# The first batch's attention as float32 matmuls on 64 x 64 quarters of the array, two heads at once

## The chip, the cores and the metric

The program runs on one NeuronCore of a Trainium2 chip. The metric is the device time of one execution in microseconds, median of several runs; lower is better. In the text PE is TensorE, PEld its weight loads, ACT is ScalarE, DVE is VectorE, POOL is GpSimd, and SP is the engine that issues nearly all DMAs of this kernel.

## What is computed

Three stages follow one another: a sigmoid attention, a gated feed-forward block behind an RMS norm, and a top-1 mixture of eight experts. The change touches the first stage alone, and of that the first of four batches.

```python
# q, k, v: (4 batches, 12 heads, 448 tokens, 64), float32
def _attn_ref(q, k, v):
    scores = np.matmul(q, k.transpose(0, 1, 3, 2)) / np.sqrt(64) - np.log(448)
    return np.matmul(1.0 / (1.0 + np.exp(-scores)), v)

def _moe_ref(x, w_gate, w_val, w_out, rms_g):     # x: (1792, 768), d_ff 1536
    xn = x / np.sqrt(np.mean(x * x, axis=-1, keepdims=True) + 1e-06) * rms_g
    g = xn @ w_gate
    return (g / (1.0 + np.exp(-g)) * (xn @ w_val)) @ w_out
# then _moe2_ref: logits = x @ w_gate; the best expert's relu(x @ w1) @ w2, times its probability
```

## The kernel before

One program in an order written out by hand issues everything; every engine works through its own queue in that order. The four batches pass through two stages that overlap. `attention(b)` is a generator whose steps are one chunk of keys of one head (12 heads, NC = 4 chunks of 128 keys, the last one of 64). `moe1(b)` is the feed-forward block of a batch in steps of nine matmuls, and between its steps it calls steps of the next batch's attention. The first batch's attention has nothing to run beside, so it stands alone at the start of the program, and beside it run the conversions of the first twelve chunks of the feed-forward weights (HELD = 12).

**Queries and keys.** `load_qk` fetches a head's 128 x 960 tile `rqk` (480 KB): the 64 dimensions of its queries and keys, twice over, one copy under the other. `prep` makes three things of it: an ACT cast of the whole tile to the matmul type float32r (`qkh`, L528), a DVE subtraction that puts the queries' rest into the lower 64 partitions (L530), and a DVE subtraction for the keys' rest (`kl`, L532). `scores` then runs two float32r matmuls for a chunk, L556 and L557, over all 128 rows.

**Values.** In the first batch `whole` is true for all six pairs of heads: the weights `a` and the raw values `rv` (352 KB for a pair, padded with zeros so that two heads share one 128-column result) go into plain float32 matmuls, L602 for a full chunk and L604 for the two short chunks of a pair at once. `combine_pair` copies the result to `xt` by ACT (L636), and `squares` adds its squares to `ss` (ACT L630, DVE L631).

**Weights.** `load_64` fetches one of the 36 chunks of 768 KB as 64-bit words into one of three buffers, `narrow` makes float32 of it in three DVE operations (L227, L231, L235). The load for the third chunk after it is queued on SP some ticks behind the last of the three. `split_w` makes of two converted chunks the operands `wh` and `wl` of the first feed-forward step (ACT L258, DVE L261).

**The end of the first attention.** When `ss` is complete, four small matmuls `pm` (L700) sum it over partitions, DVE takes the inverse root (L705 to L728), matmuls `prs` (L732) spread it over partitions, and six rounds of DVE and ACT work make the operands `xh` and `xl` of `moe1(0)`. Meanwhile the first steps of batch 1's attention are taken, one for each of these steps.

SP issues DMAs in the order of the program, and each of them waits for its buffer: a waiting DMA holds all that stand behind it.

Of the kernel before, what the change touches and what calls it, by code (L numbers as in the profile page):

```python
# [19 lines left out]
B, H, S, D = 4, 12, 448, 64  # L20
# [20 lines left out]
SP = mybir.EngineType.SP  # L41

HELD = 12
HELD_AT = (1, 1, 1, 0)

RAW = 3

# [6 lines left out]

def whole(b, p):

    return b == 0 or b == 1 and p in (0, 2, 4)


def attention_due(b, n):  # L60
# [44 lines left out]
def f32(ap):  # L105
    return ap.bitcast(F32)


@with_exitstack
def block_kernel(ctx, tc, qk, v, vw, wg, wv, wo, g, gate, w1, w2, consts, out):  # L110
    nc = tc.nc
    ctx.enter_context(tc.manual_schedule())

# [59 lines left out]
    def later(ticks, f, *a):  # L173

        due.setdefault(clock[0] + ticks, []).append((f, a))
# [42 lines left out]
    def narrow(c):  # L218

        r = w64.pop(c)  # L220
        lo, hi = r[:, :, 0], r[:, :, 1]
        if place[c] is not None:
            w = wp.tile([128, DM], F32, tag=f"h{place[c]}", name="w32h")
        else:
            w = wp.tile([128, DM], F32, tag="w32", name="w32", bufs=4)
        u = w.bitcast(I32)
        nc.vector.tensor_scalar(  # L227
            out=u, in0=hi, scalar1=3, scalar2=0x3FFFFFF8, op0=ALU.logical_shift_left, op1=ALU.bitwise_and
        )
        yield  # L230
        nc.vector.scalar_tensor_tensor(  # L231
            out=u, in0=lo, scalar=29, in1=u, op0=ALU.logical_shift_right, op1=ALU.bitwise_or
        )
        yield
        nc.vector.scalar_tensor_tensor(  # L235
            out=u, in0=hi, scalar=-0x40000000, in1=u, op0=ALU.bitwise_and, op1=ALU.bitwise_or
        )
        w32[c] = w
        if c < HELD:
            to_store.append((c, w))  # L240
        else:
# [264 lines left out]

    def load_qk(b, h):
        r = aq.tile([128, S + KW], F32, tag="rqk", name="rqk", bufs=RQK)
        nc.sync.dma_start(out=r, in_=qk[b, h])
        raw_a[b, h] = r  # L510

    raw_v = {}
# [1 line left out]
    def load_v(b, p):  # L514
        rv = aq.tile([128, VW], F32, tag="rv", name="rv", bufs=2)
        if whole(b, p):
            nc.sync.dma_start(out=rv, in_=vw[b, p])
        else:
            nc.sync.dma_start(out=rv[:, : 4 * 128], in_=v[b, p])
        raw_v[b, p] = rv  # L520
# [24 lines left out]
    def attention(b):  # L545
# [5 lines left out]
        def scores(t):  # L551
            h, c = divmod(t, NC)
            q2, kh, kl, _ = prep_a[b, h]
            psc = (mm_bank if b == 0 and t % 5 in (1, 3, 4) else sc_bank)([128, S], "psc")
# [107 lines left out]
            for f, a in steps_due.pop(now[0], []):  # L662
                f(*a)

        for t in range(n_steps + 4):
# [24 lines left out]
            next(coming, None)  # L690
            yield
# [403 lines left out]
        yield  # L1095


    load_qk(0, 0)
    load_v(0, 0)
    for h in range(1, RQK):  # L1100
        load_qk(0, h)
    for _ in prep(0, 0):
        pass
    att = {b: attention(b) for b in range(B)}
    for n in range(H * NC + 5):
        next(att[0])
        if n in (2, 4, 6):
            load_64(n // 2 - 1)
        if n == 20:
# [3 lines left out]
        if n == 30:  # L1113
# [7 lines left out]
        if n in (40, 44):  # L1121
            split_w(0, n // 4 - 10)
    ahead_of = 0
    for _ in att[0]:
        tick()
# [155 lines left out]
def _layout(q, k, v, moe_w_gate, moe_w_val, moe_w_out, moe_rms_g, moe2_w_gate, moe2_w1, moe2_w2):  # L1281
    c = np.ascontiguousarray

    words = lambda w: c(w).view(np.int64)
    cols = lambda w: words(w.reshape(KD, 128, KF, 128).transpose(2, 1, 0, 3))


    vp = v.reshape(B, H // 2, 2, S, D)
    parts = np.concatenate([vp, vp[:, :, :, 384:]], axis=3).reshape(B, H // 2, 2, 4, 128, D).transpose(0, 1, 4, 3, 2, 5)
    padded = np.zeros((B, H // 2, 128, VW // D, D), v.dtype)  # L1290
    for c3 in range(3):
        padded[:, :, :, 3 * c3 : 3 * c3 + 3 : 2] = parts[:, :, :, c3]
    padded[:, :, :64, 9] = parts[:, :, :64, 3, 0]
    padded[:, :, 64:, 10] = parts[:, :, 64:, 3, 1]

    once = np.concatenate([q, k, k[:, :, 384:]], axis=2).transpose(0, 1, 3, 2)
    return {
        "qk": c(np.concatenate([once, once], axis=2)),
        "v": c(parts).reshape(B, H // 2, 128, 4 * 128),
        "vw": padded.reshape(B, H // 2, 128, VW),  # L1300
        "wg": cols(moe_w_gate),
        "wv": cols(moe_w_val),
        "wo": words(moe_w_out.reshape(KF, 128, KD, 128).transpose(2, 1, 0, 3)),
        "g": c(moe_rms_g.reshape(KD, 128).T),
        "gate": c(moe2_w_gate.reshape(KD, 128, E).transpose(1, 0, 2)),
        "w1": c(moe2_w1),
        "w2": c(moe2_w2),
        "consts": CONSTS,
    }
# [17 lines left out]
```

## Time and profile before

| | us |
|---|---|
| three runs | 1013.36, 1014.91, 1015.14; median 1014.91 |
| the profiled execution | 1011.73 |
| its span, first to last instruction | 1009.9 |
| first score matmul of batch 0 | 6.17 |
| last value matmul of batch 0 issued | 60.4 |
| `pm` of batch 0 | 65.07 |
| `moe1(0)` in dense work from | 72.8 |

The profile has a busy time for each engine, a chain of work followed back from the last instruction, groups of equal instructions with their mean time, and a timeline. A matmul's record is longer than the time that it keeps the array, since consecutive ones overlap; how long it keeps the array is the distance from one start to the next. A plain float32 matmul leaves two records, a float32r matmul one. PE is in work all through: what can be won is what shortens the stretch before 72.8 us, or makes PE's work less.

### The profile page before, as it was taken

How to read it: one execution, taken by the hardware profiler on the slowest of the kernel's cores; microseconds unless marked ns; L12 is line 12 of the kernel's file. 1: busy time of each engine (PE TensorE's matmuls, PEld its weight loads, DVE VectorE, ACT ScalarE, POOL GpSimd, SP SyncE). 2: the span in 40 equal slices, each digit the busy share in tenths (PEclk: the TensorE clock that was granted, in tenths of full speed). 3: DMA queues.
4: the chain of work that ended last, by engine and by line, in shares of the span. 5: the costliest groups of instructions: out<-in, count | busy, mean ns of one | idle time of the engine just before them, and what ended most of it. 6: DMA issues, size and time to landing. Idle time of an engine off the chain costs nothing.

```text
span 1009.9 us, 13971 instructions
## 1 busy us (share of the span) xinstructions
PE 980.6 (97%) x4998; PEld 868.8 (86%) x4998; DVE 676.1 (67%) x1172; ACT 511.1 (51%) x845; POOL 14.9 (1%) x43
## 2 busy tenths in 40 slices
PE   7989999998999999999999999999999999999995
PEld 5658988897899999989999999999898878889994
DVE  5889987897789785678878465654445834434453
ACT  6865766643788883478888333333322132232230
POOL 0000000010000000000000100000000000000000
PEclk9999999999999999999999999999999999999998
DMA  8987863686735345564432469433576649839542
GB/s 312 348 291 283 322 209 111 221 251 201 229 97 179 112 130 147 168 193 125 151 128 79 142 196 341 126 98 125 152 220 236 183 138 363 296 104 304 156 73 40
DMA packets 123120, 191.48 MB, mean 190 GB/s; under 512 B 62665, under 2 KB 79817, under 8 KB 123040
## 3 DMA queue, kind: packets, MB, share of 16 engines
q1 hardware_dynamic: 122896, 189.95, 58.0%
q8 instruction: 41, 0.67, 0.3%
q0 software_dynamic: 144, 0.53, 0.2%
q14 instruction: 39, 0.32, 0.1%
HBM read 152.44 MB, written 37.88 MB: 188 GB/s over the span
## 4 chain that ended last, share of the span: by engine, by line
PE 89%; DVE 6%; DMA 2%; issue 1%; ACT 1%; SPq 0%; DVEq 0%; ACTq 0%
PE mm L305 20%; PE mm L307 20%; PE mm L306 19%; PE sc L305 4%; PE sc L306 4%; PE sc L307 4%; PE psc L557 3%; PE psc L556 3%; PE pav L602 3%; PE pav L611 2%; PE pav L613 2%; DMA rqk<-in_qk 1%; PE sc L969 1%; PE mm L391 1%; PE mm L945 1%
## 5 line engine op out<-in xcount | busy, mean ns | idle before, releaser
L305 PE MATMUL mm<-xh,wh 128*128 128x448 f32 x576 | 218.3, 379 | 0.5 <-DVE sg L314 0.3
L306 PE MATMUL mm<-xl,wh 128*128 128x448 f32 x576 | 210.6, 366 | 0.2 <-DVE xl L735 0.2
L307 PE MATMUL mm<-xh,wl 128*128 128x448 f32 x576 | 210.8, 366 | 0.0
L261 DVE TENSOR_TENSOR wl<-w,wh 128x768 fp32r<-128x768 f32 x126 | 119.4, 948 | 26.1 <-ACT wh L258 22.5
L258 ACT CAST wh<-w 128x768 fp32r<-128x768 f32 x126 | 105.5, 837 | 53.8 <-PE mm L306 27.5
L305 PEld LDWEIGHTS mm<-xh,wh 128*128 128x128 f32 x576 | 108.2, 188 | 14.6 <-issue 3.3
L306 PEld LDWEIGHTS mm<-xl,wh 128*128 128x128 f32 x576 | 108.2, 188 | 12.5 <-issue 3.5
L307 PEld LDWEIGHTS mm<-xh,wl 128*128 128x128 f32 x576 | 108.2, 188 | 8.6
L572 ACT ACTIVATE a<-psc,logs 128x448 f32<-128x448 f32 x153 | 97.5, 638 | 34.6 <-PE psc L557 30.3
L305 PE MATMUL mm<-hs,wh 128*128 128x448 f32 x288 | 106.5, 370 | 0.3 <-DVE xr L352 0.3
L307 PE MATMUL mm<-hs,wl 128*128 128x448 f32 x288 | 106.0, 368 | 0.1
L306 PE MATMUL mm<-hs,wh 128*128 128x448 f32 x288 | 105.8, 367 | 0.0
L576 ACT ACTIVATE ah<-psc,logs 128x448 fp32r<-128x448 f32 x120 | 76.2, 635 | 0.0
L556 PE MATMUL psc<-qkh 128*128 128x448 f32 x164 | 67.1, 409 | 8.0 <-DVE qkh L530 6.2
L307 PE MATMUL mm<-xd,w1l 128*128 128x448 f32 x192 | 70.3, 366 | 1.9 <-DVE w1l L804 1.9
L305 PE MATMUL sc<-hh,w2h 128*128 128x448 f32 x192 | 70.5, 367 | 1.6 <-DVE s_ti L1013 1.6
L818 ACT ACTIVATE hh<-mm 128x448 fp32r<-128x448 f32 x32 | 17.4, 544 | 106.3 <-PE mm L307 106.3
L305 PE MATMUL mm<-xd,w1h 128*128 128x448 f32 x192 | 70.9, 369 | 0.0
L306 PE MATMUL mm<-xd,w1h 128*128 128x448 f32 x192 | 70.1, 365 | 0.0
L306 PE MATMUL sc<-hl,w2h 128*128 128x448 f32 x192 | 69.7, 363 | 0.0
L307 PE MATMUL sc<-hh,w2l 128*128 128x448 f32 x192 | 69.6, 363 | 0.0
L589 DVE TENSOR_TENSOR al<-a,ah 128x448 fp32r<-128x448 f32 x90 | 55.8, 620 | 11.3 <-ACT ah L576 9.5
(207 smaller groups left out, 1660.0 us busy)
## 6 DMA issues: line engine op xcount, KB each, us to landing
w<-w32d SPq DMA_DIRECT2D x108, 384.0 KB, 4.0
rqk<-in_qk SPq DMA_DIRECT2D x48, 480.0 KB, 4.1
w1r<-in_w SPq DMA_DIRECT2D x24, 512.0 KB, 7.4
w2r<-in_w SPq DMA_DIRECT2D x32, 384.0 KB, 6.5
x2s<-x2s SPq DMA_DIRECT2D x48, 224.0 KB, 2.0
xd<-x2s SPq DMA_DIRECT2D x8, 1344.0 KB, 10.4
w<-in_wg SPq DMA_DIRECT2D x12, 768.0 KB, 6.5
w<-in_wv SPq DMA_DIRECT2D x12, 768.0 KB, 6.0
```

The lines of the kernel that those rows point to most:

```text
L258: nc.scalar.copy(out=h, in_=w3)
L261: nc.vector.tensor_tensor(out=l, in0=w3, in1=f32(h), op=ALU.subtract)
L305: nc.tensor.matmul(p, wh, xh, start=(n == 0), stop=False)
L306: nc.tensor.matmul(p, wh, xl, start=False, stop=False)
L307: nc.tensor.matmul(p, wl, xh, start=False, stop=last)
L556: nc.tensor.matmul(psc, kh[:, keys], q2, start=True, stop=False)
L557: nc.tensor.matmul(psc, kl[:, keys], q2, start=False, stop=True)
L572: nc.scalar.activation(out=a, in_=psc, bias=logs, **act)
L576: nc.scalar.activation(out=ah, in_=psc, bias=logs, **act)
L589: nc.vector.tensor_tensor(out=al, in0=a, in1=f32(ah), op=ALU.subtract)
L602: nc.tensor.matmul(pav[p], rv[:, o : o + 128], a, start=(c == 0 and j == 0), stop=False)
L611: nc.tensor.matmul(pav[h], v2[:, c, :], ah, start=(c == 0), stop=(c == 3))
```

## The change

Batch 0 leaves `scores`, `values` and `prep`, and gets `first_batch` instead, a loop over 6 pairs and 4 chunks of keys (24 steps and two for the end). Batches 1 to 3 keep their code.

A pair's tile now holds one head's queries and keys in the upper 64 partitions and the other head's in the lower 64, once each: `qk0`, 128 x 896, 448 KB for two heads. Nothing is cast. A step's `quarters` multiplies float32 queries by float32 keys in matmuls of 64 rows and 64 columns: head x uses rows 64x to 64x+63, half a chunk i of keys uses columns 64i to 64i+63, so four matmuls name four different quarters of the array. Head x writes bank x. For the last, short chunk there are two matmuls, and both write one bank, its upper and its lower half. `weights` takes the sigmoid of each bank (ACT). `weighted`, two steps later, multiplies by the raw values in the same way, half a chunk of keys on each row half and a head on each column half; the two row halves have a bank each, and `both` adds the two (ACT copy L726, DVE addition L727). The padded copies of the values are no longer read for batch 0 (256 KB instead of 352 KB for a pair).

The loop over batch 0 has 26 steps instead of 53. The conversions are spread over them, three operations in two steps, so that all twelve chunks still stand inside. The load behind a conversion is queued two ticks later instead of three. The loads of batch 1's first two heads are queued at steps 20 and 24.

The diff, cut to its core:

```diff
 def whole(b, p):
-    return b == 0 or b == 1 and p in (0, 2, 4)
+    return b == 1 and p in (0, 2, 4)
...
         if x < 2 * NU:
-            later(3, load_64, order[x])
+            later(2 if c < HELD else 3, load_64, order[x])
...
+        def first_batch():
+            raw, val, sums, score, weight = {}, {}, {}, {}, {}
+            mm = [m[:, :S] for m in fixed["mm"]]
+            n = H // 2 * NC
+            halves = [slice(0, D), slice(D, 2 * D)]
...
+            def quarters(t):
+                p, c = divmod(t, NC)
+                r = raw[p]
+                banks = [sc_bank([128, S], "psc") for x in range(2)] if c % 2 == 0 else mm[: 1 + (c < NC - 1)]
+                for x, h in enumerate(halves):
+                    for i, o in enumerate(halves):
+                        if c < NC - 1:
+                            k = S + 128 * c + D * i
+                            to = banks[x][o]
+                        elif i == x:
+                            k = S + 128 * c
+                            to = banks[0][o]
+                        else:
+                            continue
+                        nc.tensor.matmul(to, r[h, k : k + D], r[h, :S], start=True, stop=True)
+                score[t] = banks
...
+            def weighted(t):
+                p, c = divmod(t, NC)
+                if c == 0:
+                    sums[p] = [av_bank([128, S], "pav") for i in range(2)] if p % 2 == 0 else [mm[2], mi_bank([128, S], "pav")]
+                a = weight.pop(t)
...
+                        nc.tensor.matmul(
+                            sums[p][i][h], v4[o, c, x, :], a[x if c < NC - 1 else 0][o],
+                            start=(c == 0), stop=(c == (NC - 1 if i == x else NC - 2)),
+                        )
+                if c == NC - 1:
+                    then(1, both, p)
+
+            def both(p):
+                one, two = sums.pop(p)
+                nc.scalar.copy(out=xt[p], in_=one)
+                then(1, lambda: nc.vector.tensor_tensor(out=xt[p], in0=two, in1=xt[p], op=ALU.add))
+                then(2, squares, p)
...
+                    quarters(t)
+                if t == n:
+                    load_qk(1, 1)
+                    coming = prep(1, 0)
+                if t >= 2:
+                    weighted(t - 2)
+                step()
+                if t < n:
+                    weights(t)
+                next(coming, None)
...
-    for n in range(H * NC + 5):
+    for n in range(H // 2 * NC + 2):
         next(att[0])
-        if n in (2, 4, 6):
-            load_64(n // 2 - 1)
+        if n < RAW:
+            load_64(n)
...
-        if n >= 5 and len(w32) < HELD and HELD_AT[n % 4]:
-            next(conv)
+        for _ in range(1 + n % 2 if n >= 2 else 0):
+            if len(w32) < HELD:
+                next(conv)
```

On PE in the middle of batch 0's attention a stretch before reads as follows (`psc` and `mm` are score banks, `pav` is the sum over values):

```order
L556 MATMUL psc_177<-qkh_142 128x448
L557 MATMUL psc_177<-qkh_142,kl_143 128x448
L602 MATMUL pav_168<-a_153,rv_128 128x448
L556 MATMUL mm_0_123<-qkh_142 128x448
L557 MATMUL mm_0_123<-qkh_142,kl_143 128x448
```

The same place of PE now, a full chunk of a pair and the values of an earlier one:

```order
L691 MATMUL psc_261<-rqk_193 64x448 x2
L691 MATMUL psc_262<-rqk_193 64x448 x2
L717 MATMUL mm_2_125<-a_240,rv_161 64x448
L717 MATMUL pav_234<-a_240,rv_161 64x448
L717 MATMUL mm_2_125<-a2_242,rv_161 64x448
L717 MATMUL pav_234<-a2_242,rv_161 64x448
```

A score step was two float32r matmuls for one head, and is now four float32 quarters for two heads; a value step was one float32 matmul for one head, and is now four quarters for two.

On DVE, the end of batch 0's attention before, from the last operation of the eleventh chunk to the first one behind `pm` (`w32h_593` is the twelfth chunk, `qkh_607` the preparation of batch 1's second head):

```order
L235 SCALAR_TENSOR_TENSOR w32h_569<-w64_499,w32h_569 128x768
L227 TENSOR_SCALAR w32h_593<-w64_537 128x768
L231 SCALAR_TENSOR_TENSOR w32h_593<-w64_537,w32h_593 128x768
L235 SCALAR_TENSOR_TENSOR w32h_593<-w64_537,w32h_593 128x768
L530 TENSOR_TENSOR qkh_607<-rqk_546,qkh_607 64x448
L631 TENSOR_TENSOR ss_248<-ss_248,sq_610 128x448
L532 TENSOR_TENSOR kl_608<-rqk_546,qkh_607 128x512
L705 TENSOR_SCALAR va_639<-pm_627 112x4
```

And now (`w32h_555` is the twelfth chunk, `qkh_574` the preparation of batch 1's second head):

```order
L226 TENSOR_SCALAR w32h_555<-w64_488 128x768
L529 TENSOR_TENSOR qkh_552<-rqk_469,qkh_552 64x448
L230 SCALAR_TENSOR_TENSOR w32h_555<-w64_488,w32h_555 128x768
L234 SCALAR_TENSOR_TENSOR w32h_555<-w64_488,w32h_555 128x768
L531 TENSOR_TENSOR kl_553<-rqk_469,qkh_552 128x512
L727 TENSOR_TENSOR xt_137<-pav_515,xt_137 128x448
L529 TENSOR_TENSOR qkh_574<-rqk_545,qkh_574 64x448
L630 TENSOR_TENSOR ss_138<-ss_138,sq_577 128x448
L801 TENSOR_SCALAR va_604<-pm_592 112x4
```

The last sum of squares stood behind one preparation of batch 1, and now stands behind one and a half and behind the addition of the two banks.

On ACT, the same place now (`qkh_574` is again the cast for batch 1's second head, `psc_571` a score bank of batch 1):

```order
L704 ACTIVATE aj_540<-mm_0_123,logs_85 128x448
L527 CAST qkh_552<-rqk_469 128x960
L726 COPY xt_137<-mm_2_125 128x448
L527 CAST qkh_574<-rqk_545 128x960
L629 ACTIVATE sq_577<-xt_137 128x448
L571 ACTIVATE a_582<-psc_571,logs_85 128x448
```

The square that ends `ss` stands behind the cast of `rqk_545`, as it stood behind that of `rqk_546` before; what moved is the load of that tile, which SP issues now behind the last score step of batch 0, because it takes over the last pair's buffer.

## Rows read from the trace of the kernel before

**Rows 1.** Windows by stage: busy us and count by engine, granted clock, DMA share, GB/s.

```profile
core 0: us, PE busy (x) PEld busy (x) DVE busy (x) ACT busy (x) POOL busy (x), PEclk, DMA share, GB/s
30.00:50.00 20.00, 20.00 (x72) 12.87 (x70) 18.29 (x28) 17.33 (x30) 0.00 (x0) 1.00 1.00 351
60.80:72.80 12.00, 9.02 (x36) 5.51 (x35) 9.82 (x26) 6.86 (x11) 0.00 (x0) 0.86 0.86 297
72.80:240.00 167.20, 166.90 (x797) 147.47 (x797) 150.45 (x230) 99.72 (x168) 5.05 (x12) 1.00 0.66 230
```

**Rows 2.** Timeline of PE: start us, us; batch 0's first matmuls, then one step.

```profile
6.17 0.74 PE L556 MATMUL psc<-qkh 128*128 128x448 f32 x1 [6.17 <-DVE qkh L530]
...
7.81 0.57 PE L557 MATMUL mm<-qkh,kl 128*128 128x448 f32 x1
...
12.11 0.36 PE L557 MATMUL psc<-qkh,kl 128*128 128x448 f32 x1
...
36.03 0.71 PE L556 MATMUL mm<-qkh 128*128 128x448 f32 x1
...
36.78 0.91 PE L602 MATMUL pav<-a,rv 128*128 128x448 f32 x2
37.18 0.72 PE L556 MATMUL mm<-qkh 128*128 128x448 f32 x1
```

**Rows 3.** Timeline of PE's weight loads while only float32 value matmuls run.

```profile
58.52 0.19 PEld L602 LDWEIGHTS pav<-a,rv 128*128 128x128 f32 x1 [0.19 <-issue]
58.89 0.19 PEld L602 LDWEIGHTS pav<-a,rv 128*128 128x128 f32 x1 [0.19 <-issue]
```

**Rows 4.** A late stage on 32 columns each: its group, and the chain there.

```profile
L945 PE MATMUL mm<-wf,xt 128*32 128x256 f32 x48 | 2.8, 381 | 0.0
...
823.97 2.73 PE mm L945 x48
```

**Rows 5.** Groups of ACT from 0 to 66 us: busy us, mean ns, idle before.

```profile
L528 ACT CAST qkh<-rqk 128x960 fp32r<-128x960 f32 x14 | 13.9, 990 | 6.0 <-DMA rqk<-in_qk 5.9
L572 ACT ACTIVATE a<-mm,logs 128x448 f32<-128x448 f32 x21 | 12.9, 630 | 0.6 <-PE mm L557 0.5
...
L636 ACT COPY xt<-pav 128x448 f32<-128x448 f32 x6 | 3.2, 534 | 5.3 <-PE pav L604 5.3
...
L630 ACT ACTIVATE sq<-xt 128x448 f32<-128x448 f32 x5 | 2.9, 570 | 0.0
```

**Rows 6.** Groups of DVE from 0 to 66 us.

```profile
L235 DVE SCALAR_TENSOR_TENSOR w32h<-w,w32h 128x768 int32<-128x768 int32 x12 | 11.5, 958 | 0.3
L231 DVE SCALAR_TENSOR_TENSOR w32h<-w,w32h 128x768 int32<-128x768 int32 x12 | 11.4, 952 | 0.0
L532 DVE TENSOR_TENSOR kl<-rqk,qkh 128x512 fp32r<-128x512 f32 x14 | 9.6, 686 | 0.1
L530 DVE TENSOR_TENSOR qkh<-rqk,qkh 64x448 fp32r<-64x448 f32 x14 | 8.7, 622 | 12.1 <-ACT qkh L528 11.6 <-PE mm L557 0.4
L227 DVE TENSOR_SCALAR w32h<-w 128x768 int32<-128x768 int32 x12 | 6.7, 560 | 1.7 <-DMA w<-in_wg 1.2 <-DMA w<-in_wv 0.2
```

**Rows 7.** DMA from 12 to 60 us: total, and one issue group with time to landing.

```profile
DMA packets 4521, 17.08 MB, mean 356 GB/s; under 512 B 761, under 2 KB 761, under 8 KB 4518
...
rqk<-in_qk SPq DMA_DIRECT2D x10, 480.0 KB, 5.1
```

**Rows 8.** Chain of work, first piece: start us, us.

```profile
0.76 3.70 DMA rqk<-in_qk
```

**Rows 9.** Timeline at the end of batch 0's attention.

```profile
61.90 0.99 ACT L528 CAST qkh<-rqk 128x960 fp32r<-128x960 f32 x1
62.66 0.96 DVE L235 SCALAR_TENSOR_TENSOR w32h<-w,w32h 128x768 int32<-128x768 int32 x1
...
63.95 0.47 PE L556 MATMUL psc<-qkh 128*128 128x448 f32 x1 [1.83 <-ACT a L572]
...
65.07 0.92 PE L700 MATMUL pm<-ones,ss 128*112 128x1 f32 x8 [0.45 <-DVE ss L631]
```

More of the change, by code (lines that the diff above doesn't have):

```diff
@@ L43 @@
 HELD = 12
-HELD_AT = (1, 1, 1, 0)
 RAW = 3
@@ L109, in block_kernel @@
 @with_exitstack
-def block_kernel(ctx, tc, qk, v, vw, wg, wv, wo, g, gate, w1, w2, consts, out):
+def block_kernel(ctx, tc, qk0, qk, v, vw, wg, wv, wo, g, gate, w1, w2, consts, out):
     nc = tc.nc
@@ L508, in load_qk @@
         r = aq.tile([128, S + KW], F32, tag="rqk", name="rqk", bufs=RQK)
-        nc.sync.dma_start(out=r, in_=qk[b, h])
+        nc.sync.dma_start(out=r, in_=qk[b - 1, h])
         raw_a[b, h] = r
@@ L516, in load_v @@
         if whole(b, p):
-            nc.sync.dma_start(out=rv, in_=vw[b, p])
+            nc.sync.dma_start(out=rv, in_=vw[p // 2])
         else:
@@ L553, in scores @@
             q2, kh, kl, _ = prep_a[b, h]
-            psc = (mm_bank if b == 0 and t % 5 in (1, 3, 4) else sc_bank)([128, S], "psc")
+            psc = sc_bank([128, S], "psc")
             keys = slice(128 * c, 128 * c + 128)
@@ L663, in step, with load_pair, weights @@
                 f(*a)
-        for t in range(n_steps + 4):
+        def first_batch():
[3 more added lines that the diff above has]
+            halves = [slice(0, D), slice(D, 2 * D)]
+            def load_pair(p):
+                raw[p] = aq.tile([128, S + KW], F32, tag="rqk", name="rqk", bufs=RQK)
+                nc.sync.dma_start(out=raw[p][:, : 2 * S], in_=qk0[p])
+            def quarters(t):
[14 more added lines that the diff above has]
+                score[t] = banks
+            def weights(t):
+                act = dict(func=AF.Sigmoid, bias=logs, scale=1.0 / math.sqrt(D))
+                weight[t] = []
+                for i, p in enumerate(score.pop(t)):
+                    if t % NC == NC - 1:
+                        a = f32(aq.tile([128, S], F32R, tag="al", name="aj", bufs=3))
+                    elif i == 0:
+                        a = aq.tile([128, S], F32, tag="a", name="a", bufs=4)
+                    else:
+                        a = f32(aq.tile([128, S], F32R, tag="ah", name="a2", bufs=4))
+                    nc.scalar.activation(out=a, in_=p, **act)
+                    weight[t].append(a)
+            def weighted(t):
[3 more added lines that the diff above has]
+                a = weight.pop(t)
+                v4 = raw_v[0, p][:, : 4 * 128].rearrange("s (c j d) -> s c j d", j=2, d=D)
+                for x, h in enumerate(halves):
+                    for i, o in enumerate(halves):
+                        if c == NC - 1 and i != x:
+                            continue
+                        nc.tensor.matmul(
[9 more added lines that the diff above has]
+                then(2, squares, p)
+            load_pair(0)
+            load_v(0, 0)
+            load_pair(1)
+            fresh()
+            coming = iter(())
+            for t in range(n + 2):
+                p, c = divmod(t, NC)
+                if t < n:
+                    if c == 0 and 0 < p < H // 2 - 1:
+                        load_pair(p + 1)
+                    if c == 0 and p == H // 2 - 1:
+                        load_qk(1, 0)
+                    if c == 2:
+                        nb, np = (0, p + 1) if p + 1 < H // 2 else (1, 0)
+                        load_v(nb, np)
+                    quarters(t)
[5 more added lines that the diff above has]
+                step()
+                if t < n:
+                    weights(t)
+                next(coming, None)
+                yield
+            for _ in coming:
+                pass
@@ L666, in attention @@
+        if b == 0:
+            yield from first_batch()
+        for t in range(n_steps + 4 if b else 0):
             if t < n_steps:
@@ L1095, in all_slots @@
         yield
[L1098 to L1103, printed above, removed]
     att = {b: attention(b) for b in range(B)}
-    for n in range(H * NC + 5):
+    for n in range(H // 2 * NC + 2):
         next(att[0])
-        if n in (2, 4, 6):
-            load_64(n // 2 - 1)
-        if n == 20:
+        if n < RAW:
+            load_64(n)
+        if n == 10:
             nc.sync.dma_start(out=cst, in_=consts)
@@ L1112, in block_kernel @@
             nc.sync.dma_start(out=gate_sb, in_=gate)
-        if n == 30:
+        if n == 15:
             nc.scalar.copy(out=gate_2[:, :, :E], in_=gate_sb)
@@ L1117, in block_kernel @@
             )
-        if n >= 5 and len(w32) < HELD and HELD_AT[n % 4]:
-            next(conv)
+        for _ in range(1 + n % 2 if n >= 2 else 0):
+            if len(w32) < HELD:
+                next(conv)
         tick()
-        if n in (40, 44):
-            split_w(0, n // 4 - 10)
+        if n in (20, 22):
+            split_w(0, n // 2 - 10)
     ahead_of = 0
@@ L1294, in _layout @@
     padded[:, :, 64:, 10] = parts[:, :, 64:, 3, 1]
-    once = np.concatenate([q, k, k[:, :, 384:]], axis=2).transpose(0, 1, 3, 2)
+    once = np.concatenate([q, k, k[:, :, 384:]], axis=2).transpose(0, 1, 3, 2)[1:]
+    pairs = np.concatenate([q[0], k[0]], axis=1).reshape(H // 2, 2, 2 * S, D).transpose(0, 1, 3, 2)
     return {
+        "qk0": c(pairs).reshape(H // 2, 128, 2 * S),
         "qk": c(np.concatenate([once, once], axis=2)),
         "v": c(parts).reshape(B, H // 2, 128, 4 * 128),
-        "vw": padded.reshape(B, H // 2, 128, VW),
+        "vw": c(padded.reshape(B, H // 2, 128, VW)[1, ::2]),
         "wg": cols(moe_w_gate),
```

## The prediction

> **What bounds the kernel now.** I read the windows by stage first, then PE's timeline inside the first attention, then the groups of ACT and DVE there, and last the end of that attention. The windows [rows 1] say three things. From 72.8 us on PE is busy 166.90 of 167.20 us at the full granted clock, so whatever makes that stretch begin earlier moves all behind it by as much, and nothing in it gives more. From 60.8 to 72.8 us PE is busy 9.02 of 12 us: a chain of small steps. And between 30 and 50 us, inside batch 0's attention, four resources are nearly full at once: PE 20.00 of 20 us, DVE 18.29, ACT 17.33, and the DMA engines at share 1.00 with 351 GB/s. An edit that lightens one of the four gives little there; this one has to be followed on all four.
>
> **PE.** One step before takes 37.18 - 36.03 = 1.15 us [rows 2]: two float32r matmuls of 0.20 and one float32 matmul of 0.75, whose two halves lie 58.89 - 58.52 = 0.37 apart [rows 3]. A pair of heads cost 8 x 2 x 0.20 = 3.2 for scores and 7 x 0.75 = 5.25 for values, 8.45 us; six pairs 50.7. Now a full chunk of a pair is four float32 quarters for scores and four for values. What four of them cost together, no row shows for 64 x 64 tiles. The nearest one is a float32 stage on 32 columns [rows 4]: 48 records in 2.73 us, 57 ns a record. Alone a record of 256 columns would keep the array 256/448 x 0.375 = 0.21 us, so four column groups do run at the same time there, with 6% lost. If quarters do the same in both directions, four of them take the time of one, 0.75 us, and with that loss at most 0.80; I take 0.76. If only the columns overlap, and not the rows, it is 1.5. A short chunk has two quarters, and takes as long as four. So a pair is 8 x 0.76 = 6.1 instead of 8.45 us, and six pairs 36.5: 14.2 us less work. I take this end since the row nearest to it has overlapping tiles of the same data type; the other end is a rival below.
>
> The page TensorEngine Tiling (Array Packing) of the Trainium skill, section Key Properties, states that tiles of one mode load weights and multiply in parallel, and its configurations name 64x64 with four tiles; by it the step is the 0.76 that I take, and no run here shows the row direction.
>
> **ACT.** Per pair before: 8 sigmoids of 0.63, two casts of 0.99, copy 0.53, square 0.57 [rows 5], 8.1 us. Now 7 sigmoids, copy, square: 5.5 us. The twelve casts go (two for batch 1 stay). That is under PE's 6.1, though not by much, and its slack is one step: scores are written two steps ahead.
>
> **DVE.** The two subtractions of a head, 0.69 + 0.62, go twelve times: -15.7 us [rows 6]. One addition per pair comes, priced as the 0.62 of a subtraction: +3.7 us. The conversions stay, 12 x (0.56 + 0.95 + 0.96) = 29.6 us. With sums of squares (5 x 0.62), two halves of `split_w` (0.95 each, as an L231) DVE has 29.6 + 3.7 + 3.1 + 1.9 = 38.3 us. It can begin when the first weights land, at about 8 us (1.9 MB queued ahead and with them), so it ends near 46.4.
>
> **DMA and SP.** Two heads cost 448 + 256 KB instead of 960 + 352 KB. Queued up to and with the load of batch 1's second head are 6 x 448 + 6 x 256 KB, 13 chunks of 768 KB, 324 KB of constants, 2 x 480 and 352 KB for batch 1: 16.2 MB. From 2 us on at 351 [rows 1] to 356 GB/s [rows 7] that is 47.6 to 48.2. The queue on SP is moved too: that last load waits for the last scores, since it reuses their buffer, and behind it wait the following weight load and batch 1's third head.
>
> **The new wait.** A pair's square (ACT) now needs DVE's addition, which stands behind conversions in DVE's queue; behind the square stand the next sigmoids, and for those PE waits. The addition of pair p stands behind 2p+2 chunks; DVE reaches it at about 8 + 3.2(2p+2), that is 14.4 + 6.4p, and PE reaches the step that is held at about 17.5 + 6.1p. The margin is 3 us at the start and 1.5 at the last pair, so I cost it at nothing, with 1.5 us for the range.
>
> **The sum.** PE starts when the first tile lands, 0.76 + 3.70 = 4.46 [rows 8], a little less for the smaller tile: 4.4 instead of 6.17. The array begins at the lower granted clock: a record of 0.57 at 7.81 against 0.36 at 12.11 [rows 2]. If the clock rises at the same time as before, near 11.5, seven microseconds at half speed cost 3.5. Up to the last scores there are 24 score steps and 21 value steps: 45 x 0.76 = 34.2; with 0.5 for the first banks, 4.4 + 3.5 + 34.2 + 0.5 = 42.6. The load of batch 1's second head is issued then and lands 5.1 us later [rows 7], 47.7; by bytes 48.2. I take the later. Before, the cast of that tile ended at 62.89 and `pm` came 2.18 us behind it, because PE had to wait for a sigmoid before the scores ahead of `pm` [rows 9]; the order there is the same now. So 48.2 + 1.0 + 2.2 = 51.4. The path over DVE gives less: conversions end at 46.4 (before 63.62 [rows 9]), then key subtraction 0.69, addition 0.62, square 0.57, a sigmoid 0.63 and scores of some 0.9, 49.8 with signals about 50. So `pm` moves from 65.07 to 51.4, 13.7 us. What follows is the same code; PE idles somewhat longer ahead of it, so the low clock of that stretch (0.86 in [rows 1]) may last a little longer, for which I take 0.2 off: **13.5 us**. On the profiled execution's 1011.73 that is 998.2; the median of the three runs lies 3.18 above it, and 1014.91 - 13.5 = 1001.4 is what I predict. It isn't given back behind: from 72.8 us PE is full, and DMA share there is 0.66.
>
> **Rivals.**
> Row halves do not overlap (slower). Then each of the 45 steps takes 1.5: 4.4 + 3.5 + 67.5 = 75.4 for the last scores, + 5.1 + 1.0 + 2.2 = 83.7 for `pm`, 18.6 us later than before: 1033.5. It decides from 1.06 us a step, where the gain is gone. Against it: [rows 4] show tiles of the other direction overlapping almost fully. For it: no row has 64-row tiles side by side. 8%.
>
> The clock stays low through the quarters (slower). The array works at 1.2 GHz until the first stage behind: 4.4 + 45 x 1.5 = 71.9, `pm` at 80.2, 1030. For it: before, the low level held for the first five microseconds of PE's work [rows 2]; against it: PE is as closely filled with work as before. 4%.
>
> One bank, two row halves. Both quarters of a short score chunk write one bank. If they are kept apart, six steps take 0.75 longer: 4.5 us less gain, 1006. It is a reading of the program alone; in the trace no such pair stands. 5%.
> That different row tiles may not use one PSUM bank at the same time is stated by the Trainium skill, page TensorEngine Tiling (Array Packing), section Restrictions and Gotchas; by it the short score chunk is the one place at risk, and the time would be the 1006 of this rival.
>
> The four queues catch on each other. ACT 5.5, DVE 6.4, DMA 2.3 MB/0.351 = 6.5 and PE 6.1 us a pair lie so close that each wait on one is a wait on all; at 7.2 us a pair, a loss of 1.1 us each on PE, the gain is 7 us: 1008. 6%.
>
> **How the numbers follow.** The forecast, a gain of 9 to 18 us, has 77%; the bank 5%, the queues 6%, the row halves 8%, the clock 4%. A difference under 0.2% (2 us) can't be told from none; the queues would have to cost twice as much for it, so of theirs and of the others' chance I give it 3%. Faster 85%, same 3%, slower 12%. The range holds the forecast, the bank and most of the queues: from 996.5 (clock up at once and loads at 390 GB/s, `pm` near 47) to 1010 (a step of 0.94 instead of 0.76).
>
> **What would show it.** Right: the L691 and L717 groups start four records within a few tens of ns and one step of both every 1.5 us; L704 ends each pair in under 6 us; the cast of batch 1's second head waits for its DMA and ends near 49; `pm` near 51.4; the windows behind are as before, 13 us earlier. Wrong: records of the lower rows that begin only when those of the upper end; records of twice the length with a clock under 1; DVE waits of ACT L629 longer than 1.5 us; or a stretch behind `pm` that is longer than before.

## The result and the profile after

| | before | after |
|---|---|---|
| median of four runs side by side, us | 1014.13 | 998.42 (997.95 to 998.65) |
| ratio after to before, 95% interval | | 0.9847 [0.9832, 0.9862] |
| the profiled execution; its span | 1011.73; 1009.9 | 997.95; 996.1 |
| first score matmul | 6.17 | 4.25 |
| first conversion of weights begins | 13.32 | 9.39 |
| last value matmuls of batch 0 begin | 60.39 | 43.55 |
| last of the twelve conversions ends | 63.62 | 49.33 |
| cast of batch 1's second head ends | 62.89 | 49.20 |
| `pm` | 65.07 | 52.56 |
| first matmul of `moe1(0)` | 71.91 | 60.74 |

The kernel became 15.7 us faster; 13.5 were predicted. The forecast of 1001.4 us missed the time by 3.0, and 998.4 lies inside the range of 996.5 to 1010. Of the 3.0 us, 2.2 are the gain and 0.8 the start: the forecast counted from 1014.91, and the runs of before beside those of after have 1014.13. The windows of after by stage answer to [rows 1] (columns as there):

```profile
14.00:42.00 28.00, 27.44 (x257) 13.56 (x254) 24.70 (x35) 23.15 (x44) 0.00 (x0) 1.00 0.98 355
30.00:40.00 10.00, 10.00 (x100) 4.67 (x92) 9.76 (x14) 7.81 (x15) 0.00 (x0) 1.00 0.97 359
46.00:60.00 14.00, 10.30 (x31) 7.92 (x32) 9.86 (x26) 5.32 (x8) 0.00 (x0) 0.51 0.86 308
60.00:225.00 165.00, 164.52 (x782) 144.57 (x782) 148.47 (x227) 98.84 (x166) 5.05 (x12) 1.00 0.65 225
```

Four resources are nearly full together, as before: in 30 to 40 us PE 10.00, DVE 9.76 of 10 us, DMA share 0.97 at 359 GB/s. The third row is new: through the chain of small steps at the end of the stage the granted clock is 0.51, so nearly all of it runs at 1.2 GHz, where [rows 1] had 0.86. Behind it PE is full again at 2.4 GHz, and nothing is given back there.

PE's timeline answers to [rows 2]: the first scores, then a full step and a short one (start us, record us; x8 are eight records, that is four quarter matmuls; a record shows the bank's name, `mm` or `psc`, without its number):

```profile
4.25 1.77 PE L691 MATMUL psc<-rqk 64*64 64x448 f32 x8 [4.25 <-DMA rqk<-in_qk]
5.79 1.72 PE L691 MATMUL mm<-rqk 64*64 64x448 f32 x8
...
16.56 1.29 PE L691 MATMUL psc<-rqk 64*64 64x448 f32 x8
...
21.42 0.54 PE L691 MATMUL mm<-rqk 64*64 64x448 f32 x1
21.43 0.59 PE L717 MATMUL pav<-a,rv 64*64 64x448 f32 x1
21.44 0.54 PE L691 MATMUL mm<-rqk 64*64 64x448 f32 x1
...
22.57 1.29 PE L691 MATMUL psc<-rqk 64*64 64x448 f32 x8
...
23.32 1.28 PE L717 MATMUL pav<-a,rv 64*64 64x448 f32 x8
...
24.07 1.28 PE L691 MATMUL mm<-rqk 64*64 64x448 f32 x8
...
25.18 0.54 PE L717 MATMUL pav<-aj,rv 64*64 64x448 f32 x1
25.19 0.59 PE L691 MATMUL psc<-rqk 64*64 64x448 f32 x2
25.20 0.91 PE L717 MATMUL pav<-aj,rv 64*64 64x448 f32 x3
```

Four quarters cost 23.32 - 22.57 = 0.75 us, exactly what one full float32 matmul costs [rows 2]; at the lower clock, at the start, 1.54. Around 25.19 values and scores of neighbouring steps begin within 20 ns: a short chunk takes only the quarters that it names, and the next step's matmuls fill the others. Even so the pair whose scores begin at 16.56 is followed by the next one at 22.57: 6.01 us, eight times 0.75.

The end of batch 0's attention in after answers to [rows 9]:

```profile
48.21 0.99 ACT L527 CAST qkh<-rqk 128x960 fp32r<-128x960 f32 x1 [3.13 <-DMA rqk<-in_qk]
48.37 0.96 DVE L234 SCALAR_TENSOR_TENSOR w32h<-w,w32h 128x768 int32<-128x768 int32 x1
...
49.24 0.69 DVE L531 TENSOR_TENSOR kl<-rqk,qkh 128x512 fp32r<-128x512 f32 x1
...
49.84 0.62 DVE L727 TENSOR_TENSOR xt<-pav,xt 128x448 f32<-128x448 f32 x1
...
50.50 0.58 ACT L629 ACTIVATE sq<-xt 128x448 f32<-128x448 f32 x1 [1.30 <-DVE xt L727]
...
51.65 0.74 PE L555 MATMUL psc<-qkh 128*128 128x448 f32 x1 [0.18 <-ACT a L571]
...
52.56 1.51 PE L796 MATMUL pm<-ones,ss 128*112 128x1 f32 x8
```

ACT's cast waits 3.13 us for the load and ends at 49.20, which is the forecast's 49.2. But the chain into `pm` does not pass through it: the last conversion, key subtraction, addition, square, sigmoid, scores follow on each other from DVE's queue. `pm` takes 1.51 against 0.92 [rows 9]: the clock again.

### The profile page after: what moved, and what is told of

The parts are those of the page before. It is cut to its first block, busy times and chain, and to the rows that moved or that the text cites. A ratio compares the mean times of both kernels' runs of the same rounds, so it can differ in the third digit from the quotient of the medians.

```text
span 996.1 us, 14209 instructions
## 1 busy us (share of the span) xinstructions
PE 965.7 (97%) x5154; PEld 852.9 (86%) x5154; DVE 664.9 (67%) x1154; ACT 496.5 (50%) x827; POOL 14.8 (1%) x43
## 4 chain that ended last, share of the span: by engine, by line
PE 90%; DVE 6%; DMA 1%; issue 1%; ACT 1%; SPq 0%; DVEq 0%; ACTq 0%
PE mm L304 20%; PE mm L306 20%; PE mm L305 20%; PE sc L304 4%; PE sc L305 4%; PE sc L306 4%; PE psc L555 3%; PE psc L556 3%; PE pav L610 2%; PE pav L612 2%; PE pav L601 1%; PE sc L1065 1%; PE mm L1041 1%; PE mm L390 1%; PE psc L691 1%
## 5 line engine op out<-in xcount | busy, mean ns | idle before, releaser
L571 ACT ACTIVATE a<-psc,logs 128x448 f32<-128x448 f32 x138 | 88.2, 640 | 31.3 <-PE psc L556 27.5
L304 PEld LDWEIGHTS mm<-hs,wh 128*128 128x128 f32 x288 | 54.1, 188 | 6.4 <-issue 0.5
```

Of the source, the lines that this page charges most:

```text
L304: nc.tensor.matmul(p, wh, xh, start=(n == 0), stop=False)
L571: nc.scalar.activation(out=a, in_=psc, bias=logs, **act)
```

## The experiments

**The theory:** four quarters run as one matmul, and the gain comes because PE, DVE and the loads are all lightened; at the end DVE's queue delivers last. **The rivals:** the row halves do not really overlap and the gain is that of the casts and subtractions left out; or the earlier start of loads and conversions makes the gain; or one of the queues alone sets the end and the others don't matter. The table has every run; times of the stage are read from the one profiled execution of each kernel, so up to 0.7 us between two rows need not come from the edit (the first pair's addition, far ahead of the edits of fill and tail, comes at 14.67 us in after, at 15.00 in fill and at 15.35 in tail). Each ratio is to runs of before on the same chip, and their medians differ: 1014.13 beside after, 1013.40 beside one_half, dve_back, act_back and fill, 1013.56 beside pe_back, dma_back, w0_gate and best, 1013.11 beside before_early and tail. So costs and gains below are taken from the ratios; 0.1% is 1.0 us.

| kernel | median, us | ratio to before [95%] | first conversion | last one ends | `pm` | first `moe1` |
|---|---|---|---|---|---|---|
| before | 1014.13 | 1 | 13.32 | 63.62 | 65.07 | 71.91 |
| after | 998.42 | 0.9847 [0.9832, 0.9862] | 9.39 | 49.33 | 52.56 | 60.74 |
| one_half | 1078.54 | 1.0643 [1.0623, 1.0662] | 9.35 | 126.7 | 133.4 | 141.2 |
| pe_back | 1019.68 | 1.0059 [1.0041, 1.0077] | 9.17 | 70.87 | 74.11 | 81.92 |
| dve_back | 1008.20 | 0.9951 [0.9936, 0.9966] | 9.75 | 59.95 | 63.18 | 71.36 |
| dma_back | 1003.62 | 0.9895 [0.9875, 0.9914] | 10.44 | 55.35 | 59.50 | 67.12 |
| act_back | 999.65 | 0.9866 [0.9851, 0.9881] | 9.40 | 50.14 | 53.37 | 60.83 |
| before_early | 1014.91 | 1.0019 [1.0009, 1.0028] | 11.87 | 66.3 | 67.75 | 74.39 |
| w0_gate | 997.89 | 0.9838 [0.9818, 0.9857] | 6.09 | 50.06 | 53.30 | 61.24 |
| tail | 997.61 | 0.9849 [0.9834, 0.9864] | 9.49 | 50.00 | 53.24 | 61.42 |
| fill | 996.94 | 0.9838 [0.9823, 0.9852] | 9.56 | 49.65 | 52.50 | 59.15 |
| best | 995.42 | 0.9822 [0.9807, 0.9837] | 6.16 | 47.34 | 50.19 | 56.61 |

### Only one row half (one_half)

```diff
-                        nc.tensor.matmul(to, r[h, k : k + D], r[h, :S], start=True, stop=True)
+                        nc.tensor.matmul(to, r[halves[0], k : k + D], r[halves[0], :S], start=True, stop=True)
...
-                            sums[p][i][h], v4[o, c, x, :], a[x if c < NC - 1 else 0][o],
+                            sums[p][i][h], v4[halves[0], c, x, :], a[x if c < NC - 1 else 0][halves[0]],
```

> Both heads of a pair multiply on the same 64 rows of the array (the lower row half is left idle, so the second head's scores and the second half of the keys' values are replaced by copies of the first); the two column halves still work side by side. Count of matmuls, shapes, banks, ACT, DVE and DMA work are those of the changed kernel. If the gain on PE comes from row halves that work at the same time, a full chunk takes 1.5 instead of 0.75 us in scores and in values: 6 x 3 x 2 x 0.75 = 27 us more work on PE, which has some 4 us of slack against DVE: pm near 76 instead of 52.6, about 1021 us. If row halves never overlapped, nothing changes: 998. If PE had far more slack than its records show: under 1010.

Measured: 1078.54 against the 1021 expected, 80 us slower than after. PE's timeline of one_half inside the stage, and at its end:

```profile
41.63 3.25 PE L691 MATMUL psc<-rqk 64*64 64x448 f32 x8
44.62 1.76 PE L717 MATMUL mm<-a,rv 64*64 64x448 f32 x4
46.11 1.76 PE L717 MATMUL pav<-a,rv 64*64 64x448 f32 x4
...
136.05 0.57 PE L555 MATMUL psc<-qkh 128*128 128x448 f32 x1
136.42 0.57 PE L556 MATMUL psc<-qkh,kl 128*128 128x448 f32 x1
...
142.16 0.36 PE L306 MATMUL mm<-xh,wl 128*128 128x448 f32 x1
142.36 0.36 PE L304 MATMUL mm<-xh,wh 128*128 128x448 f32 x1
```

The eight records of a score step keep PE 44.62 - 41.63 = 2.99 us, against 1.54 at the lower clock in after. So with the same rows for all, two quarters stand behind two others: the row halves of after do work at the same time. The other factor of two is the clock. At 136 us starts of float32r matmuls lie 0.37 apart, at 142 us 0.20: up to 139.3 us this kernel ran at 1.2 GHz, although PE had no gap (38.00 of 38 us busy from 42 to 80 us, and none from its first matmul at 4.2 to 131.8). The clock column shows 1.00 there, since no change of the level is on record ahead of it; the spacing is the evidence. So the miss in size is the clock, which with one row half idle did not rise.

### One resource given back at a time

pe_back puts one full float32 matmul ahead of each of the 24 score steps, 18 us of array work:

```diff
+                nc.tensor.matmul(banks[0], ones, r[:, :S], start=True, stop=True)
```

> The changed kernel with one float32 matmul of 128 rows, 128 columns and 448 elements ahead of each step's scores, into the bank that the scores overwrite: 24 x 0.75 = 18 us of PE work given back, about what the quarters saved, DVE, ACT and DMA as changed. Theory (PE, DVE and the loads lie so close that each alone can hold the first stage): PE needs 5.25 + 3.0 + some switching, about 8.5 us a pair, the last values end near 58 instead of 44.4, pm comes near 63 and the time is 1007 to 1011. Rival (DVE alone sets the end, PE has slack to spare): under 1002.

```profile
30.82 1.02 PE L681 MATMUL psc<-rqk,ones 128*128 128x448 f32 x2
31.77 0.98 PE L692 MATMUL psc<-rqk 64*64 64x448 f32 x8
32.57 0.93 PE L718 MATMUL pav<-a,rv 64*64 64x448 f32 x8
33.43 1.02 PE L681 MATMUL mm<-rqk,ones 128*128 128x448 f32 x2
```

A step in this timeline of PE is 33.43 - 30.82 = 2.61 us, which is 0.75 + 0.75 + 0.75 and 0.36 more. In the chain of waits of the same kernel the full matmul stands with 0.95 and the quarters behind it with 0.91, so about 0.2 at each passage. `moe1(0)` begins 21.2 us later than in after, and the kernel is slower than before, with DVE and the loads as light as in after. The expected 1007 to 1011 was missed by 9 us: a pair takes 4 x 2.61 = 10.4 us instead of the expected 8.5, so 24 x 1.11 = 26.6 us of PE's time were returned and not 18. That is more than the change took off PE, and the run says only that PE's part is needed, not how much of the gain it is.

dve_back returns the twelve pairs' subtractions, on scratch (15.7 us of DVE); act_back twelve casts of 128 x 896; dma_back fetches 608 KB more for each pair (3.6 MB), into scratch:

```diff
+                if t < n:
+                    r = raw[p]
+                    z = aq.tile([128, KW], F32R, tag="kl", name="kl", bufs=2)
+                    if t % 2:
+                        nc.vector.tensor_tensor(out=z, in0=r[:, :KW], in1=r[:, S - 64 : 2 * S], op=ALU.subtract)
+                    else:
+                        nc.vector.tensor_tensor(out=z[D:, :S], in0=r[D:, :S], in1=r[D:, S : 2 * S], op=ALU.subtract)
```

> The changed kernel with the 24 removed DVE operations given back as work on scratch (12 subtractions of 64x448 and 12 of 128x512, 15.7 us), PE, ACT and DMA as changed; nothing waits for their results. Theory: behind the change DVE's queue sets the end of the first stage, so pm moves by 13 to 16 us and nearly the whole gain is gone: 1011 to 1014. Rival, PE or the loads set the end and DVE has slack: under 1004.

```diff
+                if t < n and t % 2 == 0:
+                    z = aq.tile([128, S + KW], F32R, tag="qkh", name="qkh", bufs=2)
+                    nc.scalar.copy(out=z[:, : 2 * S], in_=raw[p][:, : 2 * S])
```

> The changed kernel with 12 casts of 128x896 to scratch on ACT given back (about 0.93 us each, 11.2 us), one for each two steps, PE, DVE and DMA as changed. Theory (DVE sets the end, ACT has 1 us of slack in each pair of 6.4 us): ACT needs 7.4 us a pair and becomes the bound, 6 x 1.0 = 6 us, less what DVE's tail hides: plus 3 to 7 us, 1001 to 1005. Rival, ACT was the bound already: plus 11, 1009. Rival, ACT has room: 998 to 999.

```diff
+                nc.sync.dma_start(out=raw[p][:, 2 * S :], in_=qk[2, p, :, : KW - S])
...
+                        z, y = (wp.tile([128, DM], F32, tag="w32", name="w32", bufs=4) for _ in range(2))
+                        nc.sync.dma_start(out=z, in_=qk[2, p, :, : DM])
+                        nc.sync.dma_start(out=y[:, :192], in_=qk[2, p, :, DM :])
+                        if nb == 0:
+                            nc.sync.dma_start(out=raw_v[nb, np][:, 4 * 128 :], in_=qk[2, p, :, : VW - 4 * 128])
```

> The changed kernel with the bytes that it no longer loads fetched again into scratch, 608 KB a pair of heads (3.6 MB, 10.3 us at 355 GB/s), nobody waits for them but the queue; PE, ACT and DVE as changed. Theory (the loads lie as close as PE and DVE): the weights land later by most of that, DVE waits for them, pm moves by 7 to 10 us and the time is 1005 to 1009. Rival (the loads had slack behind DVE): under 1002.

Groups of DVE in dve_back from 5 to 62 us, the work returned:

```profile
L753 DVE TENSOR_TENSOR kl<-rqk 128x512 fp32r<-128x512 f32 x12 | 8.3, 691 | 0.0
L755 DVE TENSOR_TENSOR kl<-rqk 64x448 fp32r<-64x448 f32 x11 | 6.8, 623 | 0.3
```

From the list of waits in dma_back (us in total, times, longest):

```profile
DVE w32h L226 <- DMA w<-in_wg: 15.4, 5, 9.4
...
PE psc L692 <- DMA rqk<-in_qk: 11.2, 5, 4.2
```

The subtractions cost 0.9951 - 0.9847 = 1.04%, 10.5 us of their 15.7; `moe1(0)` begins 10.6 us later. The rest went into DVE's idle time: three of them (1.9 us) run before the first conversion, and of the 2.8 us of waits within its work 0.2 are left. The loads cost 0.48%, 4.9 us of 10.3; beside the 9.4 us for its first chunk DVE waits 6.0 us for weights of the gate matrix, where after has 0.8, and PE waits 11.2 us for the pairs' tiles, where after has 0.6. The casts cost 0.19%, 1.9 us of 11.2, and the two intervals overlap: ACT had room, as the forecast of 5.5 us a pair said. All three were expected to cost more: 1011 to 1014 was written down for dve_back, 1005 to 1009 for dma_back, 1001 to 1005 for act_back, and each came out between its theory and its rival. So none of PE, DVE and loads sets the time alone: 10 us are lost if DVE gets its work back, 5 if the loads do, and 21 with PE's heavier return.

### The earlier start

before_early gives the kernel before the early weight loads of the change alone:

```diff
-        if n in (2, 4, 6):
-            load_64(n // 2 - 1)
+        if n < RAW:
+            load_64(n)
```

> The kernel before with the first three weight loads queued at steps 0, 1 and 2 instead of 2, 4 and 6, as the changed kernel has them; nothing else. Theory (the gain comes from the work taken off PE, DVE and the loads, not from the earlier start of the conversions): 0 to 2 us less, 1011.5 to 1013.5. Rival (the earlier start is the main part): 6 us or more less, under 1008.

Its list of waits, to be held against the idle times of L530 and L528 in [rows 6] and [rows 5], 11.6 and 5.9 us:

```profile
DVE qkh L530 <- ACT qkh L528: 15.9, 10, 4.2
...
ACT qkh L528 <- DMA rqk<-in_qk: 10.3, 6, 3.2
```

Conversions begin 1.45 us sooner and end 2.7 us later; the time is 0.19% (1.9 us) longer, where 0 to 2 us less were expected. Heads' tiles come later, since weights stand ahead of them in the queue; ACT waits 10.3 us for them, DVE 15.9 us for ACT. The early start alone gives nothing. The rest of the new schedule, loads queued two ticks behind a conversion instead of three and conversions spread over fewer steps, was not run alone.

w0_gate asks the same of after. It loads the first chunk of weights right behind the first pair's tile, and moves a subtraction for the gate, which held DVE for 0.9 us, two ticks back:

```diff
             load_pair(0)
+            load_64(0)
             load_v(0, 0)
...
-            nc.vector.tensor_tensor(
+            later(2, lambda: nc.vector.tensor_tensor(
```

> The changed kernel with two edits on DVE's queue alone: the first weight chunk is loaded right behind the first pair's tile, ahead of its values and the second pair's tile, so that DVE can start near 7 instead of 9.4 us; and the small subtraction of the gate's weights, which held DVE for 0.9 us behind ACT, is put two ticks later. Theory (DVE's queue sets the end): conversions end 2 to 3 us earlier, until the load of batch 1's second head binds (its cast ended at 49.2): pm earlier by 1 to 1.5 us, 997.2. Rival (the loads bind with DVE): no difference, 998.4.

DVE's waits in w0_gate, from 5 to 50 us:

```profile
DVE w32h L226 <- DMA w<-in_wg: 7.8, 3, 5.0
...
DVE xt L727 <- ACT xt L726: 2.5, 2, 2.1
...
DVE w32h L226 <- DMA w<-in_wv: 1.3, 1, 1.3
```

And in after:

```profile
DVE w32h L226 <- DMA w<-in_wg: 9.1, 2, 8.3
...
DVE gate L1205 <- ACT gate L1204: 0.9, 1, 0.9
DVE w32h L226 <- DMA w<-in_wv: 0.8, 1, 0.8
```

Without the first, longest wait DVE idles 2.8 + 1.3 + 2.5 = 6.6 us inside its work here, and in after 0.8 + 0.9 + 0.8 and 0.3 more for an addition, 2.8. It starts 3.3 us sooner and ends no earlier (0.7 us later in this execution): it runs ahead of PE and of the loads and then waits for both. The median, 997.89, lies between theory and rival, and its interval [0.9818, 0.9857] holds after's ratio, so the trace decides: `pm` came at 53.30, not 1 to 1.5 us earlier. The theory that DVE's queue alone sets the end, which dve_back had spoken for, fell with this run. The loads wait for DVE in turn. Of SP's waits in after, from 5 to 50 us, the longest in total is that for a weight buffer to be converted and free:

```profile
SPq L214 <- DVE w32h L234: 19.5, 10, 4.1
```

With three buffers, weights and conversions wait for each other. What that costs is open, since the DMA engines are at share 0.98 from 14 to 42 us all the same; a fourth buffer was not tried.

### The end of the stage

tail queues three weight loads later, so that batch 1's second head is fetched ahead of them:

```diff
-            later(2 if c < HELD else 3, load_64, order[x])
+            later(6 if HELD <= x < HELD + 3 else 2 if c < HELD else 3, load_64, order[x])
```

> The changed kernel with one edit: the three weight loads behind the twelfth chunk are queued six ticks instead of two behind their conversion, so that the load of batch 1's second head stands ahead of them on SP. Theory (the end of the first stage is held by DVE's queue and by that load together): the cast of batch 1's second head ends 3 us earlier, near 46, DVE as before near 49.3, pm earlier by less than 1 us, 997.6 to 998.4. Rival (the load alone held it): pm near 50, 996 or less.

Its timeline there:

```profile
46.81 0.99 ACT L527 CAST qkh<-rqk 128x960 fp32r<-128x960 f32 x1 [1.05 <-DMA rqk<-in_qk]
...
49.04 0.96 DVE L234 SCALAR_TENSOR_TENSOR w32h<-w,w32h 128x768 int32<-128x768 int32 x1
...
53.24 0.58 PE L796 MATMUL pm<-ones,ss 128*112 128x1 f32 x3
```

The cast ends 1.4 us sooner (47.80), `pm` comes 0.7 us later, with the conversion ahead of it. The load was not what `pm` waited for. The median of 997.61 lies in what the theory expected, but the ratio is after's (0.9849 and 0.9847), so nothing was won.

The table says the same of every kernel with these queues: in after, pe_back, dve_back, act_back, w0_gate and tail `pm` comes 3.23 or 3.24 us behind the end of the last conversion, whenever that is, and 2.85 in fill and best, which have the fillers told of below. (It is 4.15 in dma_back and 6.7 in one_half, where other waits lie between.)

fill keeps PE at work through the waits there, with eight float32 matmuls of constants whose result nobody reads:

```diff
+            for _ in range(4):
+                nc.tensor.matmul(mm[1], ones, cst[:, :S], start=True, stop=True)
```

and three and one more of them between the first scores of batch 1.

> The changed kernel with eight float32 matmuls of 128x448 that nobody reads, put on PE where it waits at the end of batch 0's attention: four behind the last values, three between the two halves of batch 1's first score chunk, one behind its second. Theory: the low granted clock from 46.1 to 59.7 us comes from PE's wait there and costs 1.3 us in the small steps behind it (pm 1.51 instead of 0.92 us and so on); with the wait filled the clock holds and the time falls by 1.0 to 1.5 us, to about 997.2. Rival, that stretch isn't bound by PE's speed: no difference, or up to 0.7 slower if the fillers delay the scores ahead of pm.

Its window over the end of the stage:

```profile
46.00:60.00 14.00, 12.43 (x48) 7.09 (x47) 11.73 (x30) 6.54 (x10) 0.00 (x0) 1.00 0.82 278
```

The granted clock is 1.00 instead of 0.51, with 2.1 us more of PE's busy time. `pm` stays (52.50), `moe1(0)` begins 1.59 us sooner: 6.65 us from `pm` to there instead of 8.18, and 6.84 before. The median of 996.94 is near the expected 997.2, but the ratios differ by 0.09% (0.9 us) and their intervals overlap: in the time the gain is not shown, in the trace it is. Between 225 and 235 us the profile of fill has a low stretch that after's has not (its window, same columns):

```profile
225.00:235.00 10.00, 7.58 (x28) 5.90 (x28) 8.93 (x14) 4.86 (x8) 0.00 (x0) 0.83 0.58 170
```

### The parts together (best)

best is w0_gate, tail and five of the fillers (two, two and one).

> Both edits of w0_gate, the three weight loads behind the twelfth chunk queued six ticks instead of two behind their conversion, so that the load of batch 1's second head comes ahead of them, and five of the eight fillers on PE that held the clock. Theory: the cast of batch 1's second head ends 2 us earlier as well, pm near 50, and the small steps behind it run at the full clock: 3 to 4 us less than the changed kernel, 994.5 to 995.5. Rival (the weights held back are missed in the feed-forward stage, or five fillers don't hold the clock): 997 or more.

Its timeline:

```profile
44.18 0.99 ACT L527 CAST qkh<-rqk 128x960 fp32r<-128x960 f32 x1 [0.36 <-DMA rqk<-in_qk]
...
46.38 0.96 DVE L234 SCALAR_TENSOR_TENSOR w32h<-w,w32h 128x768 int32<-128x768 int32 x1
...
50.19 0.95 PE L804 MATMUL pm<-ones,ss 128*112 128x1 f32 x8
```

`pm` is 2.4 us and `moe1(0)` 4.1 us earlier than in after. The median is 995.42, as expected; by the ratios that is 0.25% or 2.5 us less than after, and the intervals just overlap. Neither w0_gate nor tail moved `pm` forward alone; with both, loads and DVE end sooner together, and the clock holds. Both edits without the fillers were not run, so their parts in the 2.4 us are not told apart.

## Why the prediction was right, and where its steps were off

**Four quarters in the time of one matmul: right.** Forecast 0.76, measured 0.75; one_half excludes the rival of the row halves.

**One bank, two row halves: did not come true.** The two score matmuls of a short chunk begin within 20 ns (at 21.42 and 21.44 us in the lines above) and nothing separates them. By the Trainium skill, page TensorEngine Tiling (Array Packing), section Restrictions and Gotchas, different row tiles may not use one PSUM bank at the same time. Here the two write the upper and the lower half of its partitions, and the measurement decides: in that form they overlap.

**"A short chunk has two quarters, and takes as long as four": the sum held, the reason did not.** The next matmuls do use the free quarters, and 28 quarter matmuls alone would be 7 x 0.75 = 5.25 us a pair. But the pair from 16.56 to 22.57 took 6.01, against the forecast's 6.1, since from 20.7 to 21.4 us only two quarters had work: the weights of the short score chunk waited for a sigmoid.

```profile
21.23 0.32 PEld L691 LDWEIGHTS mm<-rqk 64*64 64x64 f32 x3 [0.41 <-ACT a L704]
```

With the waits of other pairs, the first scores of a pair come 6.4 us apart (10.20 to 35.76 for four). So the term was met partly by luck: a loss in one place made up for the short chunk's gain. DVE's additions come 7.0 us apart (14.67 to 49.84 for five), the later ones behind conversions.

**The clock at the start: off by 3 us.** It rose at 8.5, not at 11.5. PE's last scores end at 41.2 instead of 42.6, but PE was not what ended last.

**ACT under PE: right.** Eleven us of casts cost 1.9 us in act_back, within the noise.

**The new wait at nothing: right in effect.** PE waits 0.8 us for a sigmoid that stands behind the square and DVE's addition, but PE is not what ends last.

**The two paths to `pm`: this step failed.** The load path was exact (cast ends at 49.20, forecast 49.2). The DVE path was put 1.4 us ahead of it and came out behind. The term is "DVE ends near 46.4"; it ended at 49.33. It began 1.4 us later than assumed (9.39, since the first weights landed later) and idled 2.8 us in its work; it had 1.2 us less to do by then. I priced DVE as if its queue never waited, though weights, ACT's gate and the additions stand in it. tail showed that the load was not the later path. What follows the last conversion was priced well: some 3.6 us, measured 3.23. `pm` thus came at 52.56, not at 51.4. That the forecast for `pm` was only 1.2 us off is partly luck, since the path that it was taken from did not set it.

**0.2 us for a longer low clock: too small.** From `pm` to `moe1(0)` it cost 8.18 - 6.84 = 1.3 us; the level was low from 46.05 to 59.70 us. fill got 1.59 us back. The prediction had named a longer stretch behind `pm` as a sign of being wrong, and this one came.

**From 13.5 to 15.7.** By the prediction's steps `moe1(0)` should begin 13.5 us earlier; it did 11.17. The time that makes up for it lies behind, where the prediction said that nothing is won or given back. Up to 243 us the lead grows to 11.5; then the profile of before has a low stretch, from 244.0 to 247.4, that costs it 1.5 us:

```profile
240.00:250.00 10.00, 7.45 (x28) 5.81 (x27) 7.86 (x13) 3.38 (x6) 0.00 (x0) 0.83 0.64 167
```

after's profile has none, though PE waits at the same place about as long (2.0 us up to 231.3; in before 2.2 us up to 242.7). Up to the end another 0.7 us come in small pieces, 13.8 between the two profiled executions. The last 1.9 us are between these and the medians: the profiled execution of before was 2.4 under its median, that of after 0.5. Of the twelve profiled executions nine have such a low stretch of 3.4 us some 172 us behind the start of `moe1(0)`; after, tail and dve_back have none. What decides on it, and so how much of the 4.5 us belongs to the change, stays open. The source of the gain was right, its size was met partly by luck: the gain ahead of `moe1(0)` was forecast 2.3 us too large, and 4.5 us that no step of the prediction holds came on top.

**The queues catch on each other: partly.** They do (the waits above, in both directions), but PE's pairs came 6.4 us apart and not the 7.2 of that rival, and it did not cost the 1008 that was worked out for it: the end is set by the conversions, which came 2.9 us later than forecast.

## What to carry to other kernels

When several queues are nearly full together, ask for each of them what the change gives it, and test it by returning one at a time. Read in the trace whether what came back is what was taken off. An edit that lightens only one, or only starts sooner, moves the wait to another queue. A queue that works in order is not the sum of its operations: count the entries in it that wait for others. Where a faster stage ends in a chain of small steps, price that chain at the lower clock.

## What the runs showed of the hardware

- Float32 matmuls of 64 rows and 64 columns on the four quarters cost 0.75 us for 448 columns, all four together, and matmuls of different steps ran side by side on quarters that a short chunk left free, begun within 20 ns. A pair took 6.01 us all the same, as if its short chunks were full, since quarters idled behind a wait of 0.41 us for a sigmoid.
- Two quarters on the two row halves that write the upper and the lower half of one bank began within 20 ns, with no delay.
- With one row half idle through a whole stage the clock stayed at 1.2 GHz up to 139.3 us, though PE had no gap from 4.2 to 131.8 us; with all four quarters at work it rose 4.3 us after the first matmul.
- A full-array matmul between quarter matmuls cost 0.36 us more than its own 0.75. Both wrote one bank in pe_back, so whether the passage or the bank costs it was not told apart.
- Eight matmuls that compute nothing (2.1 us more of PE's busy time from 46 to 60 us) kept the clock at 2.4 GHz through the end of the stage and brought the next stage 1.59 us forward.
